# Seven-product steps from batch 5 on, one last pass for the leftover tokens of batches 4 to 7, four sums per operand, attention issued up to batch 5

## The chip, the cores and the metric

The kernel runs on one core of one Trainium2 chip. The metric is the device time of one execution in microseconds (us); lower is better. The kernel before takes 695.51 us, the median of 694.57, 695.51 and 696.79. The profile is of one further execution of 693.6 us.

## The reference

Attention over 32 memory slots, and a feed-forward layer on its output, all in fp32:

```python
a = softmax(phi, over seq)                      # 8 batches, 8 heads, 576 tokens, 32 slots
k_m, v_m = einsum('bhsm,bhsd->bhmd', a, k), einsum('bhsm,bhsd->bhmd', a, v)
p = softmax(q @ k_m.T / sqrt(64), over slots)   # 576 x 32 per head
x = (p @ v_m) laid out as 4608 tokens x 512     # 8 heads x 64
h = x @ w_in                                    # 512 -> 2048
out = gelu(h) @ w_out                           # 2048 -> 512
```

## The kernel before

A product in fp32 is made of three matmuls in the format fp32r: each operand x is split into a high part hi (a cast) and a low part lo (x - hi), and hi*hi, hi*lo and lo*hi are added up in PSUM. `copy` (line 244) makes the high parts, VectorE's subtractions the low ones. x itself is never formed: U = v_m @ w_in (`pu`, line 629, then `U` hi and lo, lines 901 and 904) is computed per batch, and the hidden layer is p @ U (`hidden`, line 945: 12 matmuls of 288 columns for 128 hidden features f of half a batch).

From batch 2 on, the work is cut into steps (batch b, half hf of its 576 tokens, pair i of the 16 blocks f). A step computes the two hidden blocks 2i and 2i+1, ScalarE applies the gelu, and one step later TensorE multiplies by the two blocks of w_out. 256 of a half's 288 tokens go through the step; the other 32 are kept in the tile `tails`. There are two kinds of product:

- A plain one (`project_half`, P): 12 matmuls of 512 columns into `acc`, fed by `gh` (the high part) and `gl` (line 977).
- A seven-product one (`seven`, S, line 1194; batches 6 and 7): Strassen's scheme on 2 x 2 blocks of 128 tokens by 256 columns. Seven products of sums of blocks, 21 matmuls of 256 columns, take the place of eight products. The sums of the gelu's blocks are made in the step on VectorE (`differences`), split by `split_hi` and `split_lo`, and `combine` adds the seven accumulators up into the output. The sums of w_out's blocks (`ws`, `wt`, `wh`, `wl`, `wz`: sum, combinations, high part, low part, store; 16 pieces spread over batches 3 to 5) are parked in DRAM, reloaded by `wi`, and `wc` swaps parts of w_out itself for its sums and back.

The leftover tokens of two batches (128 in all) go through `tg`, `tp` and `to` (split, 48 matmuls of 512 columns, output) behind batches 1, 3, 5 and 7.

The order is written out by hand. The list `START` names each piece up to batch 3 in order; behind it, `put(t, ...)` says at which half step t (32 to a batch; batch 4 is t = 128 to 159) a piece of the attention or of the weight sums is issued, `run(t)` issues what is due among the hidden blocks and gelus, and edges ("order") keep that order on each engine. A piece of step t also waits for the hidden block of half step t - 4. In names, `score` to `pl` are the attention softmax, `Up`, `Uh`, `Ul` make U, `uo` and `ui` park and reload U of batch 7, `amax` to `anorm` and `slots` prepare the memory slots of a batch. Every DMA of these stages is issued by SyncE (SP), in order.

## Time and profile before

| What | Value |
|---|---|
| median of 3 runs | 695.51 us (694.57 to 696.79) |
| profiled execution, its span | 693.6 us, 691.6 us |
| mean granted TensorE clock | 0.992 |
| TensorE busy, weight loads | 675.8 us (98%), 575.5 us (83%) |
| VectorE, ScalarE, GpSimd busy | 434.4 (63%), 375.8 (54%), 45.6 us (7%) |
| moved by DMA | 102.20 MB, mean 148 GB/s |
| chain that ended last | TensorE 88%, DMA 6%, ScalarE 2%, VectorE 2% |

Busy time says how much work an engine has; where an engine is busy all the time the others wait for it, if the chain of waits runs through it. Matmuls overlap in the pipeline, so the time of one in a group (390 ns at 512 columns) is longer than the distance between two; that distance is read from the length of a run of them in the chain, divided by their number. A granted clock of 1.00 is 2.4 GHz.

### The profile page before, as it was taken

To read this page: it belongs to the slowest core of one execution; us is meant where nothing else is said; L and a number is where in the kernel's file an instruction comes from. 1 tells how busy PE (TensorE), PEld (TensorE's weight loads), DVE (VectorE), ACT (ScalarE), POOL (GpSimd) and SP (SyncE) were. 2 spreads that over 40 slices of the span, in tenths; PEclk is the share of its full clock that TensorE was granted. 3 is DMA by queue.
4 is the path that set the end of the run, shared out by engine and by line. 5 is a ranking of instruction groups with operands and counts; after the bars stand their busy time and mean duration, and the time that the engine had idled before them with its cause. 6 is when DMAs were issued, how large, how long until landed. Compare 5 with 4: busy or idle time off the path is not lost.

```text
span 691.6 us, 13389 instructions
## 1 busy us (share of the span) xinstructions
PE 675.8 (98%) x5230; PEld 575.5 (83%) x5230; DVE 434.4 (63%) x850; ACT 375.8 (54%) x920; POOL 45.6 (7%) x38
## 2 busy tenths in 40 slices
...
GB/s 332 371 299 109 117 192 133 50 147 171 38 211 155 84 209 1 66 164 195 233 92 69 128 69 72 145 70 199 335 366 74 269 113 63 153 63 31 65 149 107
DMA packets 69378, 102.20 MB, mean 148 GB/s; under 512 B 5572, under 2 KB 43204, under 8 KB 68292
## 3 DMA queue, kind: packets, MB, share of 16 engines
...
q8 instruction: 42, 0.69, 0.4%
q14 instruction: 20, 0.16, 0.1%
...
HBM read 73.01 MB, written 28.32 MB: 147 GB/s over the span
## 4 chain that ended last, share of the span: by engine, by line
PE 88%; DMA 6%; ACT 2%; DVE 2%; issue 1%; SPq 1%; ACTq 0%; DVEq 0%
PE acc L990 35%; PE h L945 27%; PE m L1194 12%; PE tacc L990 6%; PE pu L629 4%; DMA kv<-kv 3%; PE psc L629 1%; DMA raw<-w_in 1%; DMA park<-cvr 1%; PE psc L546 1%; DMA phi<-phiT 1%; PE x L546 1%; DVE nm L436 0%; DVE gl L977 0%; DVE raw L328 0%
## 5 line engine op out<-in xcount | busy, mean ns | idle before, releaser
L945 PE MATMUL h<-p_hi,U 128*128 128x288 f32 x896 | 179.4, 299 | 0.8 <-ACT tails L964 0.5
L945 PEld LDWEIGHTS h<-p_hi,U 128*128 128x128 f32 x896 | 142.2, 188 | 21.3 <-issue 6.5
L990 PE MATMUL acc<-wo_hi,gh 128*128 128x512 f32 x384 | 150.9, 393 | 0.3 <-DVE o L244 0.2
L990 PE MATMUL acc<-wo_lo,gh 128*128 128x512 f32 x384 | 149.8, 390 | 0.0
L990 PE MATMUL acc<-wo_hi,gl 128*128 128x512 f32 x384 | 149.8, 390 | 0.0
L962 ACT ACTIVATE gf<-h 128x256 f32<-128x256 f32 x128 | 49.3, 387 | 127.5 <-PE h L945 98.7
L977 DVE TENSOR_TENSOR gl<-gf,gh 128x512 fp32r<-128x512 f32 x96 | 68.0, 710 | 58.1 <-ACT gh L244 52.4
L945 PE MATMUL h<-p_lo,U 128*128 128x288 f32 x448 | 95.4, 294 | 0.0
L990 PEld LDWEIGHTS acc<-wo_hi,gh 128*128 128x128 f32 x384 | 72.4, 188 | 17.3 <-ACT gh L244 2.5
L990 PEld LDWEIGHTS acc<-wo_hi,gl 128*128 128x128 f32 x384 | 72.1, 188 | 15.6 <-DVE gl L977 0.2
L990 PEld LDWEIGHTS acc<-wo_lo,gh 128*128 128x128 f32 x384 | 72.1, 188 | 11.9
L945 PEld LDWEIGHTS h<-p_lo,U 128*128 128x128 f32 x448 | 71.2, 188 | 0.2 <-DVE p_lo L750 0.2
L959 ACT ACTIVATE x<-h 128x256 f32<-128x256 f32 x64 | 24.6, 385 | 57.4 <-PE h L945 57.0
L904 DVE TENSOR_TENSOR U<-pu,U 128x512 fp32r<-128x512 f32 (+2 forms) x44 | 35.9, 833 | 26.6 <-ACT U L244 26.6
L1142 DVE TENSOR_TENSOR x<-x 128x256 f32<-128x256 f32 x32 | 13.6, 425 | 46.4 <-ACT x L959 46.4
L244 ACT CAST gh<-gf 128x512 fp32r<-128x512 f32 x68 | 42.4, 623 | 0.0
L1149 ACT CAST hi<-x 128x512 fp32r<-128x512 f32 x64 | 33.7, 568 | 13.5 <-DVE x L1142 13.5
L1154 DVE TENSOR_TENSOR lo<-x,hi 128x512 fp32r<-128x512 f32 x64 | 37.1, 622 | 4.8 <-ACT hi L1149 1.5
L964 ACT ACTIVATE tails<-h 128x32 f32<-128x32 f32 x192 | 37.6, 196 | 0.0
L244 ACT CAST U<-pu 128x512 fp32r<-128x512 f32 (+2 forms) x41 | 27.7, 702 | 16.0 <-PE pu L629 11.2
L1194 PE MATMUL m<-wo_lo,hi 128*128 128x256 f32 x128 | 36.1, 282 | 0.0
L1194 PE MATMUL m<-wo_hi,lo 128*128 128x256 f32 x128 | 36.1, 282 | 0.0
(159 smaller groups left out, 1086.7 us busy)
## 6 DMA issues: line engine op xcount, KB each, us to landing
...
```

What stands on the lines that cost most here:

```text
L244: return e.copy(dst, src) if e is nc.scalar else e.tensor_copy(dst, src)
L629: nc.tensor.matmul(ps[g][M * j : M * j + M], st["kT", b][rows, t, M * j : M * j + M], moving[j][rows], start=True, stop=True,)
L904: nc.vector.tensor_sub(u[:, ..., 1, :], pu, u[:, ..., 0, :].bitcast(F32))
L945: i = nc.tensor.matmul(h[:, :HS], u[g][w], x[:, g, :], start=(n == 0), stop=(n == 3 * G - 1))
L959: nc.scalar.activation(x, h[:, :n].rearrange("p (a n) -> p a n", a=2), AF.Gelu)
L962: nc.scalar.activation(gf[:, f % 2 * n : f % 2 * n + n], h[:, :n], AF.Gelu)
L964: nc.scalar.activation(t, h[:, n:HS], AF.Gelu)
L977: nc.vector.tensor_tensor(g_of("gl", *k), g_of("gf", *k), g_of("gh", *k).bitcast(F32), op=ALU.subtract)
L990: nc.tensor.matmul(acc, x, w[:, f, :], start=(first and n == 0), stop=(last and n == 2))
L1149: nc.scalar.copy(split_of("hi", b, hf, i, part), x)
L1154: nc.vector.tensor_tensor(lo, x, hi.bitcast(F32), op=ALU.subtract)
L1194: nc.tensor.matmul(acc, x, y, start=(i == 0 and k == 0 and n % 2 == 0), stop=(i == NP - 1 and k == 2), skip_group_check=True,)
```

## The change

Seven-product steps begin at batch 5, half 0 (`PS` = 10, in units of half a batch). The leftover tokens of batches 4 to 7, 256 of them, are kept (batches 6 and 7 in the tile U4) and go through a last pass of 8 seven-product steps, called batch 8: `gx` copies them into blocks on ScalarE, `combine` has six parts there and stores the quarters from two DMA queues. The scheme has four sums per operand now, not five, and fewer combinations at the end. The high and low parts of w_out share a tile `wo`, so that one of the seven products takes hi*hi and hi*lo in one matmul of 512 columns. The sums of w_out come in 8 pieces of 1024 columns, five of them written into `START` (batches 2 and 3), one each at t = 114, 140 and 147; only the right half of every second block of w_out is overwritten (`wc`, behind products of batch 4, half 1), and nothing is swapped back. The attention of all batches is issued by t = 155, U of batch 5 by t = 161: p of batches 5 to 7 and U of 6 and 7 are parked in DRAM (`po`, `uo`) and come back (`pi`, `ui`). The output copy of a plain half is on ScalarE alone from batch 3 on. The first row of the diff is one of the many rows of `START` that change.

```diff
+h.2.8.0 ws.1 wt.1 Lkv.4.1.2 Lkv.4.1.0 h.2.9.0 Lkv.4.1.4 gelu.2.8.0 Lkv.4.1.3 slotsT.3 Lkv.4.0.0
...
-    BS = 6
+    PS = 10
+    LAST_P = 4
+    LAST_U = 5
+    EARLY, OA = 8, 2
...
+            if 2 * b + hf >= PS:
                 x = blocks(b, hf, f // 2)
-                x = x[:, 2:9:6] if f % 2 else x[:, 0:2]
...
+    SUM_U = (3, "U3", "U4")
+    def w_place(i):
+        tag = SUM_U[1 + (i >= SUM_U[0])]
+        x = tile_of(
+            ("cv", tag), lambda: sb.tile([P, 2, 4, HD], F32R, tag=tag, name=f"cv_{tag}", bufs=1)
+        )
+        return x, x.bitcast(F32)
+    def w_sum(i):
+        x = w_place(i)[1]
...
+            w[:, 2 * i : 2 * i + 2].bitcast(F32).rearrange("p f n -> p (f n)")
...
+        nc.vector.tensor_tensor(x[:, 0].rearrange("p k n -> p (k n)"), hi, lo, op=ALU.add)
+    def w_sum_next(i):
+        x = w_place(i)[1]
+        w, t = x[:, 0], x[:, 1]
+        nc.vector.tensor_tensor(t[:, 0], w[:, 1], w[:, 0], op=ALU.subtract)
+        nc.vector.tensor_tensor(t[:, 2], w[:, 1], w[:, 3], op=ALU.add)
+        nc.vector.tensor_tensor(t[:, 1], w[:, 3], t[:, 0], op=ALU.add)
+        nc.vector.tensor_tensor(t[:, 3], w[:, 2], t[:, 1], op=ALU.subtract)
+    def w_sum_hi(i):
+        x, y = w_place(i)
+        nc.scalar.copy(x[:, 0], y[:, 1])
+    def w_sum_lo(i):
+        x, y = w_place(i)
+        nc.vector.tensor_tensor(x[:, 1], y[:, 1], y[:, 0], op=ALU.subtract)
+    def w_sum_out(i):
+        x = w_place(i)[1]
+        nc.sync.dma_start(park1[:, i], x[:, :, 0])
...
+            nc.sync.dma_start(park3[:, 3 * i : 3 * i + 3, w], x[:, w, 1:4])
+    def w_change(k):
+        for w, t in enumerate((wo_hi, wo_lo)):
+            t = t.bitcast(F32).rearrange("p (i x) n -> p i x n", x=2)[:, 2 * k : 2 * k + 2, 0, HD:]
+            nc.sync.dma_start(t, park1[:, 2 * k : 2 * k + 2, w])
...
+    def from_tails(i):
+        x = blocks(B, 0, i)
+        for n, t in ((0, tails(B - 1)), (1, tails(B - 3))):
+            t = t[:, 2 * i : 2 * i + 2].rearrange("p f x n -> p f (x n)")
+            if n:
+                nc.scalar.copy(x[:, 1], t[:, 0])
+                nc.scalar.copy(x[:, 0], t[:, 1])
+            else:
+                nc.scalar.copy(x[:, 2:5:2], t)
+    def differences(b, hf, i):
...
+        nc.vector.tensor_tensor(
+            x[:, 5:7], x[:, 1:2].to_broadcast([P, 2, P]), x[:, 0:3:2], op=ALU.subtract
+        )
+        nc.vector.tensor_tensor(x[:, 7], x[:, 2], x[:, 5], op=ALU.subtract)
+        nc.vector.tensor_tensor(x[:, 8], x[:, 4], x[:, 7], op=ALU.subtract)
...
         list7 = (
-            (0, 0, w(a, 1)), (0, 1, w(e, 0)), (0, 2, w(a, 0)), (0, 3, w(e, 1)),
-            (1, 0, s(1)), (1, 1, s(2)), (1, 2, s(0)),
-        )
-        m = sums_of(b, hf)
-        for n, (part, j, ws) in enumerate(list7):
-            acc = m[n // 2][:, n % 2 * HD : n % 2 * HD + HD]
+            (0, 0, s(2), m[1][:, LO]),
+            (0, 1, w(a, 0), m[2][:, LO]),
+            (0, 2, w(e, 0), m[3][:, LO]),
+            (1, 2, s(0), m[3][:, HI]),
+            (1, 1, s(1), m[0][:, LO]),
+            (1, 0, w(a, 1), m[0][:, HI]),
+            (1, 3, w(e, 1), m[1][:, HI]),
+        )
+        seen = set()
+        order = {(B, 0): (0, 4, 5, 6, 1, 2, 3), (B, NP - 1): (1, 2, 3, 4, 5, 0, 6)}
+        for n in order.get((b, i), range(7)):
+            part, j, ws, acc = list7[n]
+            bank = (1, 2, 3, 3, 0, 0, 1)[n]
             hi, lo = (split_of(v, b, hf, i, part)[:, j] for v in ("hi", "lo"))
-            for k, (x, y) in enumerate(((hi, ws[0]), (hi, ws[1]), (lo, ws[0]))):
+            three = ((acc, hi, ws[0]), (acc, hi, ws[1]), (acc, lo, ws[0]))
+            if n == 1:
+                three = ((m[2], hi, wo[:, :, a, LO]), (acc, lo, ws[0]))
+            for k, (d, x, y) in enumerate(three):
                 nc.tensor.matmul(
-                    acc, x, y,
-                    start=(i == 0 and k == 0 and n % 2 == 0),
-                    stop=(i == NP - 1 and k == 2),
+                    d, x, y,
+                    start=(i == 0 and k == 0 and bank not in seen),
+                    stop=(i == NP - 1 and k == len(three) - 1),
                     skip_group_check=True,
                 )
+            seen.add(bank)
...
+        q = o.rearrange("p a (k n) -> p (a k) n", k=2)
+        def twice(x):
+            return x.unsqueeze(1).to_broadcast([P, 2, HD])
+        def halves(x):
+            return x.rearrange("p (k n) -> p k n", k=2)
...
+            y = st["y1", b, hf] = sb.tile([P, HD], F32, tag="cols", name=f"y1_{b}_{hf}", bufs=1)
+            nc.scalar.copy(y, m[2][:, LO])
+            nc.vector.tensor_tensor(y, y, m[2][:, HI], op=ALU.add)
+        if part == 1:
+            nc.vector.tensor_tensor(q[:, 2:4], twice(st["y1", b, hf]), halves(m[3]), op=ALU.add)
+        if part == 2:
+            nc.vector.tensor_tensor(q[:, 0:4:3], twice(q[:, 3]), halves(m[0]), op=ALU.add)
+        if part == 3:
+            nc.vector.tensor_tensor(q[:, 1], q[:, 0], m[0][:, HI], op=ALU.add)
+        if b == B and part:
+            for e, k, x in ((1, 2, None), (3, 1, None), (4, 0, m[1][:, LO]), (5, 3, m[1][:, HI])):
+                if e != part:
+                    continue
+                if x is not None:
+                    nc.vector.tensor_tensor(q[:, k], q[:, k], x, op=ALU.add)
+                rows = out[(4 + k // 2 * 2) * S :][: 2 * S].rearrange("(x s) n -> x s n", s=HS)
+                rows = rows[:, 2 * P :, k % 2 * HD :][:, :, :HD]
+                by = (nc.sync, nc.scalar)[k != 2 and k != 0]
+                for y in range(2 if x is not None else 1):
+                    n = 2 if x is not None else 4
+                    by.dma_start(rows[n * y : n * y + n], q[M * n * y : M * n * (y + 1), k])
...
+        if part == 4:
+            nc.vector.tensor_tensor(q[:, 0:4:3], q[:, 0:4:3], halves(m[1]), op=ALU.add)
+            r = b * S + hf * HS
+            nc.sync.dma_start(out[r : r + 2 * P, :].rearrange("(c p) n -> p c n", p=P), o)
...
-    for b, ts in ((4, (123, 129)), (5, (150, 162)), (6, (185, 192))):
+    for b, ts in ((3, (92, 104)), (4, (119, 130)), (5, (152, 160)), (6, (138, 142)), (7, (149, 155))):
         for i, t in zip((0, 2), ts):
             put(t, f"Up.{b}.{4 * i}.4", f"Up.{b}.{4 * i + 4}.4")
             for k in range(2):
-                put(t + k, f"Uh.{b}.{4 * (i + k)}")
-                put(t + k * 1, f"Ul.{b}.{4 * (i + k)}")
-    for b, t, tq in ((4, 114, 99), (5, 142, 136), (6, 160, 152), (7, 184, 179)):
+                put(t + k, f"Uh.{b}.{4 * (i + k)}", f"Ul.{b}.{4 * (i + k)}")
...
+        (6, 133, 129, (1, 3, (0, 1, 1, 4, 4, 6, 6, 7), (1, 1, 3, 5, 6, 7, 7, 8))),
+        (7, 146, 140, (1, 3, (0, 1, 1, 3, 4, 6, 7, 7), (0, 1, 2, 3, 6, 6, 7, 8))),
...
+            if b > LAST_P:
+                put(t + lo, f"po.{b}.{hf}")
...
+            put(t + km, *heads("km", b + 2))
+    for b in range(LAST_P + 1, B):
+        for hf in range(2):
+            put(32 * b + 16 * hf - 5, f"pi.{b}.{hf}")
+    for b in range(LAST_U + 1, B):
+        for i in range(NFB):
+            put(32 * b - 16 + 4 * i + 5, f"ui.{b}.{i}")
+    put(107, "wh.4", "wl.4", "wz.4")
+    put(114, "ws.5", "wt.5")
+    put(116, "wh.5", "wl.5", "wz.5")
+    put(140, "ws.6", "wt.6")
+    put(142, "wh.6", "wl.6", "wz.6")
+    put(147, "ws.7")
+    put(148, "wt.7")
+    put(149, "wh.7", "wl.7", "wz.7")
+    put(158, *(f"wi.{k}" for k in range(IN_KV)))
+    put(159, f"wi.{IN_KV}", f"wi.{IN_KV + 1}")
+    put(162, f"wi.{IN_KV + 2}", f"wi.{IN_KV + 3}")
...
+    def ready(*k):
+        k = ".".join(map(str, k))
+        dos(f"gc.{k}.0", f"gd.{k}", f"gc.{k}.1", f"gm.{k}.0", f"gm.{k}.1")
+    def end_of(b, hf):
+        behind.append(f"C.{b}.{hf}.0")
+        behind.append(f"C.{b}.{hf}.1")
+        later.extend([[f"C.{b}.{hf}.2"], [f"C.{b}.{hf}.3"], [f"C.{b}.{hf}.4"]])
...
+        elif 2 * b + hf < PS:
             behind = [f"P.{step}"]
+            if 2 * b + hf == PS - 1 and f % 4 == 2:
+                behind += [f"wc.{f // 4}"]
             if end:
-                behind += [f"O.{b}.{hf}.{j}" for j in range(2)]
+                behind += [f"O.{b}.{hf}.{j}" + ":a" * (b > OA) for j in range(2)]
         else:
             behind = [f"S.{step}"]
-            if b == B - 1 and hf and f % 4 == 2:
-                behind += [f"wc.{f // 4}.0"]
             if end:
-                behind += [f"C.{b}.{hf}.0"]
-                later = [[f"C.{b}.{hf}.1"], [f"C.{b}.{hf}.2"], [f"C.{b}.{hf}.3", f"C.{b}.{hf}.4"]]
-        if end and b % 2 and (f == NF - 1 or b > 1 and hf):
+                end_of(b, hf)
+        if end and b in (1, 3) and (f == NF - 1 or b > 1 and hf):
             for i in range(NFB):
-                dos(f"tg.{b}.{i}")
+                dos(f"tg.{b}.{i}" + ":a" * (b > OA))
                 dos(*behind)
-                if i and later:
-                    dos(*later.pop(0))
                 behind = [f"tp.{b}.{i}"]
-                if b == BS - 1:
-                    behind += [f"wc.{i}.1"]
             behind += [f"to.{b}"]
-    dos(*behind)
+        if (b, hf, f) == (B - 1, 1, EARLY):
+            dos("gx.0")
+            ready(B, 0, 0)
+    for i in range(1, NP + 1):
+        if i < NP:
+            dos(f"gx.{i}")
+            ready(B, 0, i)
+        dos(*behind)
+        if later:
+            dos(*later.pop(0))
+        behind = [f"S.{B}.0.{i - 1}"]
+    dos(*behind, *(f"C.{B}.0.{k}" for k in range(6)))
```

Three places of the order, before and after. On TensorE, the first seven-product step of a half, of batch 6 before (`m` the accumulators; `hi`, `lo` the split sums of the gelu's blocks; `sum` the sums of w_out):

```order
L1194 MATMUL m_0_6170<-wo_hi,hi_0_0_0_6103 128x256
L1194 MATMUL m_0_6170<-wo_lo,hi_0_0_0_6103 128x256
L1194 MATMUL m_0_6170<-wo_hi,lo_0_0_0_6109 128x256
L1194 MATMUL m_0_2_6171<-sum_5677,hi_0_0_1_6107 128x256 x2
L1194 MATMUL m_0_2_6171<-sum_5677,lo_0_0_1_6111 128x256
L1194 MATMUL m_0_2_6171<-sum_5679,hi_0_0_1_6107 128x256 x2
L1194 MATMUL m_0_2_6171<-sum_5679,lo_0_0_1_6111 128x256
L1194 MATMUL m_0_3_6172<-sum_5675,hi_0_0_1_6107 128x256 x2
L1194 MATMUL m_0_3_6172<-sum_5675,lo_0_0_1_6111 128x256
```

and of batch 5 after:

```order
L1259 MATMUL m_0_5520<-sum_5370,hi_0_0_0_5453 128x256 x2
L1259 MATMUL m_0_5520<-sum_5370,lo_0_0_0_5460 128x256
L1259 MATMUL m_0_2_5521<-wo,hi_0_0_0_5453 128x512
L1259 MATMUL m_0_2_5521<-wo,lo_0_0_0_5460 128x256
L1259 MATMUL m_0_3_5522<-wo,hi_0_0_0_5453 128x256 x2
L1259 MATMUL m_0_3_5522<-wo,lo_0_0_0_5460 128x256
L1259 MATMUL m_0_3_5522<-sum_5366,hi_0_0_1_5458 128x256 x2
L1259 MATMUL m_0_3_5522<-sum_5366,lo_0_0_1_5462 128x256
L1259 MATMUL m_0_5520<-sum_5368,hi_0_0_1_5458 128x256 x2
L1259 MATMUL m_0_5520<-sum_5368,lo_0_0_1_5462 128x256
```

The products with sums come first now, and one matmul of 512 columns stands for two of 256. The accumulators are written in another order.

On VectorE, batch 4, half 0: from the low part of pair 4 (`gl_0_4`) to that of pair 6 before (in `gl_0_4` the half and the pair; `cvf` and `cvr` are the weight-sum tiles):

```order
L977 TENSOR_TENSOR gl_0_4_4486<-gf_0_4_4466,gh_0_4_4484 128x512
L1063 TENSOR_TENSOR cvr_1_4488<-cvf_1_4442,cvr_1_4488 128x5x128
L977 TENSOR_TENSOR gl_0_5_4526<-gf_0_5_4509,gh_0_5_4524 128x512
L1049 TENSOR_TENSOR cvf_0_4528<-wo_hi,wo_lo 128x512
L1053 TENSOR_TENSOR cvf_0_4528<-cvf_0_4528 128x256
L1054 TENSOR_TENSOR cvf_0_4528<-cvf_0_4528 128x256
L1055 TENSOR_TENSOR cvf_0_4528<-cvf_0_4528 128x128
L977 TENSOR_TENSOR gl_0_6_4566<-gf_0_6_4552,gh_0_6_4564 128x512
```

and after, the last twelve instructions ahead of and with the low part of pair 6 (`sT`, `smx`, `pT` belong to the softmax, `pout` is p and `Uout` U to be parked, `cv_U` the weight-sum tile; ahead of these stand, behind `gl_0_4`, two rows of each softmax sum with their two short pieces, one scaling, `gl_0_5` and two `Uout`):

```order
L928 TENSOR_TENSOR Uout_1_1_1_4697<-pu_4_1_4685,Uout_1_1_0_4696 128x512
L817 STREAM_TRANSPOSE pT_0_4727<-sT_0_4560 128x576
L811 TENSOR_TENSOR sT_1_4588<-sT_1_4588,smx_1_4702 128x576
L858 TENSOR_TENSOR pout_0_0_1_4760<-pT_0_4727,pout_0_0_0_4729 128x288
L858 TENSOR_TENSOR pout_0_1_1_4762<-pT_0_4727,pout_0_1_0_4731 128x288
L817 STREAM_TRANSPOSE pT_1_4768<-sT_1_4588 128x576
L1096 TENSOR_TENSOR cv_U_3363<-wo 128x1024
L1101 TENSOR_TENSOR cv_U_3363<-cv_U_3363 128x256
L1102 TENSOR_TENSOR cv_U_3363<-cv_U_3363 128x256
L1103 TENSOR_TENSOR cv_U_3363<-cv_U_3363 128x256
L1104 TENSOR_TENSOR cv_U_3363<-cv_U_3363 128x256
L1008 TENSOR_TENSOR gl_0_6_4796<-gf_0_6_4753,gh_0_6_4794 128x512
```

The second half of a softmax, four instructions of U, two of p and one large weight sum stand where two small pieces of a weight sum stood.

On SyncE's queue, the loads of the sums before (`parkb` keeps the parts of w_out that will be swapped):

```order
L1082 DMA parkb<-wo_hi 128x2x256 x2
L1082 DMA parkb<-wo_lo 128x2x256 x2
L1098 DMA sum_5675<-park_140 128x512
L1098 DMA sum_5677<-park_140 128x512
```

and after, the loads of p of batch 5, part of the parking of U of batch 7, a change of w_out and the first loads of sums:

```order
L840 DMA parkp_148<-pout_1_1_1_5241 128x288
L845 DMA p_hi_0_5291<-parkp_143 128x576
L845 DMA p_lo_0_5293<-parkp_143 128x576
L1145 DMA parku_142<-Uout_2_0_0_5269 128x512
...
L1145 DMA parku_142<-Uout_3_1_1_5286 128x512
L1124 DMA wo<-park_140 128x2x256 x2
L1133 DMA sum_5366<-park_139 128x512
L1133 DMA sum_5368<-park_139 128x512
```

The parking of U and p, the change of w_out and the loads of sums share one stretch of the queue; before, the changes of w_out stood behind the loads.

## Rows read from the trace of the kernel before

**Rows 1.** The page, part 1: busy time, share of the span and instructions of each engine.
```profile
PE 675.8 (98%) x5230; PEld 575.5 (83%) x5230; DVE 434.4 (63%) x850; ACT 375.8 (54%) x920; POOL 45.6 (7%) x38
```

**Rows 2.** Stretches: length, busy time per engine (instructions), granted clock, DMA share, GB/s.
```profile
340.00:420.00 80.00, 79.18 (x561) 65.68 (x560) 47.25 (x87) 39.61 (x99) 0.00 (x0) 1.00 0.30 95
460.00:480.00 20.00, 20.00 (x133) 16.39 (x132) 19.53 (x38) 15.05 (x35) 0.00 (x0) 1.00 0.44 151
480.00:500.00 20.00, 20.00 (x133) 16.43 (x132) 8.02 (x13) 9.77 (x27) 0.00 (x0) 1.00 0.94 317
500.00:520.00 20.00, 20.00 (x159) 15.84 (x158) 7.26 (x12) 7.48 (x23) 0.00 (x0) 1.00 1.04 367
560.00:660.00 100.00, 100.00 (x810) 100.00 (x808) 59.24 (x142) 52.58 (x157) 0.00 (x0) 1.00 0.20 70
```

**Rows 3.** The chain of waits in time: start us, us, engine, tile, line, instructions.
```profile
523.10 2.72 PE acc L990 x12
...
541.78 1.88 PE pu L629 x32
...
576.00 1.59 PE h L945 x12
577.60 2.49 PE m L1194 x21
...
676.56 10.92 PE tacc L990 x48
```

**Rows 4.** Timeline of the end: start us, us, engine, line, operation, output and inputs.
```profile
687.08 0.39 PE L990 MATMUL tacc<-wo_hi,gl_t 128*128 128x512 f32 x1
687.50 0.58 ACT L244 COPY to<-tacc 128x512 f32<-128x512 f32 x1 [10.40 <-PE tacc L990]
688.12 0.83 SPq L1275 DMA_DIRECT2D out<-to  x2
```

**Rows 5.** Groups on VectorE, shapes apart: count | busy us, mean ns | idle before.
```profile
L977 DVE TENSOR_TENSOR gl<-gf,gh 128x512 fp32r<-128x512 f32 x96 | 68.0, 710 | 58.1 <-ACT gh L244 52.4 <-PE pu L629 3.6
...
L1154 DVE TENSOR_TENSOR lo<-x,hi 128x512 fp32r<-128x512 f32 x32 | 22.2, 693 | 4.8 <-ACT hi L1149 1.5
L904 DVE TENSOR_TENSOR U<-pu,U 128x1024 fp32r<-128x1024 f32 x16 | 19.6, 1225 | 14.7 <-ACT U L244 14.7
L1154 DVE TENSOR_TENSOR lo<-x,hi 128x384 fp32r<-128x384 f32 x32 | 17.6, 552 | 0.0
...
L1142 DVE TENSOR_TENSOR x<-x 128x256 f32<-128x256 f32 x32 | 13.6, 425 | 46.4 <-ACT x L959 46.4
...
L807 DVE TENSOR_TENSOR sT<-sT,smx 128x576 f32<-128x576 f32 x14 | 10.6, 754 | 0.3
L795 DVE TENSOR_REDUCE smx<-sT 128x18 f32<-128x576 f32 x14 | 10.5, 749 | 3.3 <-ACT sT L791 3.2
...
L813 DVE STREAM_TRANSPOSE pT<-sT 128x576 f32<-128x576 f32 x14 | 10.3, 760 | 0.1
L1145 DVE TENSOR_TENSOR x<-x 128x128 f32<-128x128 f32 x32 | 9.1, 285 | 0.0
...
L901 DVE TENSOR_TENSOR Uout<-pu,Uout 128x512 fp32r<-128x512 f32 x8 | 5.0, 683 | 3.9 <-ACT Uout L244 3.9
```

**Rows 6.** Timeline of VectorE, batch 4: start us, us, engine, line, operation.
```profile
463.19 0.69 DVE L977 TENSOR_TENSOR gl<-gf,gh 128x512 fp32r<-128x512 f32 x1
...
473.12 0.68 DVE L977 TENSOR_TENSOR gl<-gf,gh 128x512 fp32r<-128x512 f32 x1
```

**Rows 7.** Groups on ScalarE, and one row of its timeline from 340 on.
```profile
L442 ACT ACTIVATE phi<-phi,nm 128x576 f32<-128x576 f32 x16 | 12.4, 774 | 0.7 <-DVE nm L436 0.3
...
L442 ACT ACT_TABLE_LOAD x9 | 11.5, 1283 | 0.2
...
L519 ACT ACTIVATE aT<-aT 128x1152 f32<-128x1152 f32 x6 | 6.9, 1155 | 0.0
```
```profile
345.26 0.73 ACT L1059 CAST cvr<-cvf 128x640 fp32r<-128x640 f32 x1 [4.31 <-DMA park<-cvr]
```

More of the change, by code (lines that the diff above doesn't have):

```diff
@@ L831, in p_tile, with p_part, p_out, p_in @@
         )
+    def p_part(w, b, hf, g):
+        n = 4 * hf + 2 * g + w
+        return tile_of(
+            ("pout", w, b, hf, g),
+            lambda: sb.tile([P, HS], F32R, tag=f"kv{n}", name=f"pout_{b}_{hf}_{g}_{w}", bufs=1),
+        )
+    def p_out(b, hf):
+        for g in range(G):
+            for w in range(2):
+                nc.sync.dma_start(parkp[b, hf][:, w, g], p_part(w, b, hf, g).bitcast(F32))
+    def p_in(b, hf):
+        for w in range(2):
+            t = p_tile(("p_hi", "p_lo")[w], b, hf)
+            nc.sync.dma_start(t.bitcast(F32), parkp[b, hf][:, w])
     def p_hi(b, hf, *g):
+        if b > LAST_P:
+            for x in range(G):
+                copy("a", p_part(0, b, hf, x), st["pT", b, hf][:, x])
+            return
         g = both(*g)
@@ L837, in p_lo @@
     def p_lo(b, hf, *g):
+        if b > LAST_P:
+            for x in range(G):
+                nc.vector.tensor_tensor(
+                    p_part(1, b, hf, x),
+                    st["pT", b, hf][:, x],
+                    p_part(0, b, hf, x).bitcast(F32),
+                    op=ALU.subtract,
+                )
+            return
         g = both(*g)
@@ new lines, in slot_attention_gelu_ffn @@
+    parku = [
+        dram.tile([NFB, P, G * 2 * FB], F32, tag=f"parku{b}", name=f"parku{b}", bufs=1)
+        for b in range(LAST_U + 1, B)
+    ]
+    parkp = {
+        (b, hf): dram.tile([P, 2, G, HS], F32, tag=f"parkp{b}{hf}", name=f"parkp{b}{hf}", bufs=1)
+        for b in range(LAST_P + 1, B)
+        for hf in range(2)
+    }
+    SUM_U = (3, "U3", "U4")
[5 more added lines that the diff above has]
+        return x, x.bitcast(F32)
@@ L1173, in sums_of @@
         return tile_of(("m", b, hf), make)
+    LO, HI = slice(0, HD), slice(HD, DM)
     def seven(b, hf, i):
         def w(f, half):
-            return [x[:, f, half * HD : half * HD + HD] for x in (wo_hi, wo_lo)]
+            return [x[:, f, (LO, HI)[half]] for x in (wo_hi, wo_lo)]
         def s(k):
@@ L1271, in tail_evict @@
         copy("a", o, st["tacc", b])
-        if b == B - 1:
-            for x in range(4):
-                r = (b - 1) * S + x * HS + 2 * P
-                (nc.scalar, nc.sync)[x % 2].dma_start(out[r : r + M, :], o[M * x : M * x + M])
-            return
         if b > 1:
```

374 lines of the change are left out of this document (139 added, 235 removed), and 2 rows, old and new, of the table t.

## Prediction

> **What bounds the kernel now.** I read the busy shares first: TensorE is busy 675.8 us of the span of 691.6, VectorE 434.4, ScalarE 375.8 [rows 1]. So time can come out only where TensorE's own work shrinks, and it can go in only where TensorE is made to wait. Then the stretches [rows 2]: in 340 to 420 TensorE lacks 0.82 us of 80; from 460 to 520 it lacks nothing, though VectorE is 19.53 of 20 busy in the first 20 us and the DMA engines are at 317 and 367 GB/s in the other 40; from 560 to 660 it lacks nothing, with the granted clock at 1.00 (of 2.4 GHz). Third, the chain of waits [rows 3]: it runs through TensorE alone there, one step's 12 hidden matmuls (1.59) and one step's product in turn. A plain product is 12 matmuls in 2.72 us, 0.2267 each at 512 columns; a seven-product step is 21 in 2.49, 0.1186 each at 256 columns. Last the end [rows 4]: from the end of the last matmul (687.47) there is one copy of 0.58 on ScalarE, then the issue of the last store at 688.12; the span ends 3.5 us behind that.
>
> **The change, part by part.** All sums are against the profiled execution (693.6 us, span 691.6) and are then set off from the median, 695.51.
>
> Products. The new seven-product step is 19 matmuls of 256 columns and one of 512: 19 x 0.1186 + 0.2267 = 2.48 us. Batch 5 has 16 steps that go from 2.72 to 2.48: -3.84. Batches 6 and 7 have 32 steps from 2.49 to 2.48: -0.3. The leftover tokens of batches 4 to 7 cost two passes of 48 matmuls now: 10.92 each (the second of them stands in the chain [rows 3]); in their place stand 8 steps of 2.48 = 19.84: -2.0. Together **-6.2 us**, all of it on the path. The number of attention and hidden matmuls is the same, and only their place changes.
>
> The Trainium skill has a rule against these spacings: "TensorE: Matmul & The Clock Gate", section "Back-to-back issue gap", gives N/2.4 + 2.5 ns for an isolated gap, thus 109 ns at 256 columns and 216 ns at 512, where the rows show 119 and 227. By the rule the step is 19 x 0.109 + 0.216 = 2.29, a plain step 2.59, a leftover pass 20.7 for both batch pairs, and the gain 4.8 + 2.4 = 7.2 (estimates from that page); the rows decide, and my sum stays with 6.2.
>
> End. The last matmuls no longer feed one copy. Behind them come one ScalarE copy and a row of additions on VectorE, of 256 and of 512 columns: y, then two of 512, three of 256, most of them one after the other on the same tile. The last pass orders its products so that the accumulators of the first additions close early; I count the last product's addition, and what of the earlier chain is not done by then, as four pieces of 256 columns at 0.425 [rows 5]: 1.7, against the 0.58 now. Term **+1.1** (-0.2 if only one addition is late, +2.5 if all of the chain is); the stores then take their 3.5 us as before.
>
> Batch 4, first half. Attention of batch 6 and a weight sum now stand in VectorE's queue ahead of the low part of pair 6 (gl, line 1008), for which the product waits. Between the low parts of pairs 4 and 6 stand, by rows 5: two softmax sums (2 x 0.75) with two short pieces each (4 x 0.285 at most), two scalings (2 x 0.754), two transposes (2 x 0.76), four low parts of U (4 x 0.683), two of p (2 x 0.43), gl of pair 5 (0.71), the weight sum of 1024 columns (1.225), four of its combinations at 256 columns (4 x 0.425), and gl of pair 6 itself (0.71): 13.6 us. TensorE has in that time two plain products, two sets of hidden matmuls and one U product: 2 x 2.72 + 2 x 1.59 + 1.88 = 10.5 [rows 3], and about 0.9 of lead. So gl comes 2.2 us late by lengths laid end to end. But they overlap a little: a like run of 17 instructions, from one gl to the next but one, took 9.93 us (463.19 to 473.12 [rows 6]), where the mean lengths of its groups add up to some 11.0, nine tenths. Nine tenths of 13.6 are 12.3, 0.9 more than TensorE's cover: **+0.9**, bounds 0 (row 460 to 480, where a full VectorE stopped nothing) and 2.2.
>
> Batch 3. The exponential block of ScalarE (table 1.283, two of 0.774, 1.155, table 1.283 [rows 7]) gets one more cast of 1024 columns, which I price as the 1152-column exponential, 1.155: 6.4 in all, ahead of the gelu of pair 6; a second such block follows in the second half. TensorE's cover is a plain step of 4.31 [rows 3] and the slot products, which I put at about one (a fraction of the U product's 1.88): some 5.5. **+1.0** for the two (0.3 to 1.5). In exchange the 0.82 that TensorE lacks in 340 to 420 goes: in that stretch a weight-sum cast waits 4.31 us for its parking DMA with gelus queued behind it [rows 7], and the old pieces of those sums are gone from there: **-0.8** (0 to -0.8).
>
> Batch 2. Weight sums 0 to 2 are now pinned into its steps; no wait of TensorE is seen near, and a piece of 1024 columns can hold a low part up by its own length. **+0.2**, bounds 0 and 1.2.
>
> Last pass. Its steps last 2.48 us, not 4.08, since there are no hidden matmuls left. VectorE's part of a step is 0.425 + 2 x 0.285 + 0.693 + 0.552 = 2.24 [rows 5]; ScalarE's, at the 52.58 us that 100 us of such steps (24.5) cost it now, 2.15 [rows 2]. Both fit, but they wait for each other within a step, so the loop may be as long as 2.7. One step is prepared early. **+0.3** (0 to 1.8).
>
> Nothing is put down for the change of halves, where the outputs are read out of PSUM in fewer pieces than now beside the next half's hidden matmuls, nor for the eviction on ScalarE, which is busy 54% of the span [rows 1].
>
> DMA. U of batches 6 and 7 and p of batches 5 to 7 are parked and come back. From the second half of batch 4 to batch 5's third seven-product step I count 4.2 MB of U out, 1.2 of p out, 0.6 of p in, 2.1 into the weights, 6.3 of sums in, 0.5 of output: 14.9 MB. TensorE has six plain steps, two U products and two seven-product steps in that time, 6 x 4.31 + 2 x 1.88 + 2 x 4.07 = 37.8 us, so 394 GB/s are asked for. Rows 2 show 317 and 367 for a pair of such stretches with TensorE never idle. The first eight sums are asked for two plain steps before their use and need about half of that, so I take **0**; if the whole queue were the limit at the mean 342 GB/s, 14.9 MB last 43.6: +5.8.
>
> On this the Trainium skill speaks against the change: "DMA: Bandwidth & Descriptors", section "Specifications", puts the HBM limit of one core at about 358 GB/s, below what is asked for. Row 500 to 520 shows 367 for reads and writes together, so the ceiling is about there; by the page's figure the same bytes take 41.6 us, 3.8 more than TensorE's work; if nothing could be late without harm, rival C below would give 695.8 by it.
>
> Sum: -6.2 + 1.1 + 0.9 + 1.0 - 0.8 + 0.2 + 0.3 = -3.5 us; from the median 695.5 that is **692.0 us** (690.1 against the profiled 693.6, which lies 1.9 below the median; the difference is carried over, not the level).
>
> **The rivals.** *A, all of it hidden.* VectorE's queue has slack that I don't see, as in 460 to 480, and only the end is paid: -6.2 - 0.8 + 1.1 = -5.9, 689.6 us. Against it: gl of pair 6 is queued behind more VectorE work than there is TensorE work beside it.
> *B, no change: the attention that moves into fewer batches is paid for in waits.* Batch 4, batch 3, batch 2 and the last pass at the upper part of their bounds, 2.2 + 1.5 + 0.4 + 1.0, with the end: -5.9 + 5.1 = -0.8, 694.7. For it: attention and sums of the last three batches now have to be done two batches earlier, on engines that were already full once (19.53 of 20).
> *C, slower: the DMA queue is the bound before batch 5.* One queue carries the parked U, the parked p, the changed weights and the sums in order, and the changed weights wait for the products that still read them. If the first sums arrive more than about 4 us later than I count (the lead at two plain steps, less the transfer), the first seven-product step stands still, and the delay reaches the whole difference, 5.8. Then -3.5 + 5.8 = +2.3, 697.8. For it: 394 asked for against 367 at most; against it: later loads in the queue may be late for free.
> That the seven-product steps do not pay at all is excluded by the two rows of 2.72 and 2.49.
>
> **How the numbers follow.** Forecast 0.45, A 0.16, B 0.22, C 0.17. A difference of over 0.3%, 2.1 us, can be told from no change, so faster is below 693.4. The forecast's own range, 690.6 to 693.6, lies mostly there: 0.39 faster, 0.06 same. With A, faster is 0.55. B is 0.20 same and 0.02 slower, C 0.15 slower and 0.02 same: same 0.28, slower 0.17. The range that holds 8 in 10 goes from a little under A, 689.3, to a little over C, 698.2.
>
> **What would show it.** Right: steps of line 1259 at 2.48 us and eight of them in a row at the end, in batch 5 a step of 4.07; TensorE's idle time of about 1 us each in batch 3 and in the first half of batch 4, ahead of the product of pair 6, released by gl; the last store issued some 1.8 us behind the last matmul. Wrong: a wait of a line 1259 matmul for a sum's DMA at the start of batch 5 (C); waits of several microseconds at many places of batches 2 to 4 (B); none but at the end (A); a product of 512 columns into two accumulator halves that is longer than 0.227.

## The result, and the profile after

The changed kernel takes 703.39 us, the median of four runs (702.36 to 703.85), against 695.83 for the kernel before (four runs): a ratio of 1.0108 with a 95% interval of 1.0088 to 1.0128, so 7.6 us slower. The forecast was 692.0, 3.5 us faster. The profiled execution has a span of 700.4 us.

The busy shares of the changed kernel, the page's first part, which answer to [rows 1]:

```profile
PE 675.3 (96%) x5390; PEld 581.2 (83%) x5390; DVE 461.8 (66%) x909; ACT 397.4 (57%) x978; POOL 45.6 (7%) x38
```

TensorE's busy time is all but the same, 675.3 us against 675.8, though it has fewer columns to multiply. So it was slower somewhere, and the span grew by 8.8 us beside it. The stretches (length, busy time of PE, PEld, DVE, ACT and POOL, granted clock, DMA share, GB/s), which answer to [rows 2]:

```profile
300.00:320.00 20.00, 17.86 (x162) 14.08 (x165) 9.95 (x18) 9.31 (x22) 0.00 (x0) 0.91 0.89 295
400.00:420.00 20.00, 20.00 (x153) 14.83 (x152) 12.86 (x24) 12.33 (x31) 0.00 (x0) 1.00 0.41 140
460.00:480.00 20.00, 19.32 (x141) 16.05 (x141) 10.45 (x20) 11.15 (x31) 0.00 (x0) 1.00 1.00 367
680.00:700.40 20.40, 7.66 (x62) 7.31 (x60) 7.96 (x17) 3.99 (x11) 0.00 (x0) 0.79 0.09 27
```

Two of these rows are not full. In 300 to 320 TensorE lacks 2.14 us and the clock is granted at 0.91; in the last 20.4 us it works for 7.66 only. From 400 to 420, where pair 6 of batch 4's first half lies, it lacks nothing, though the forecast had put 0.9 us there. From 460 to 480 it lacks 0.68.

The chain of waits of the changed kernel (start us, us, engine, tile, line, instructions), which answers to [rows 3]:

```profile
558.97 1.59 PE h L976 x12
560.56 2.50 PE m L1259 x20
...
572.84 2.45 PE m L1259 x20
...
662.59 25.08 PE m L1259 x200
```

A seven-product step of 20 matmuls takes 2.45 to 2.50 us, on the mean as long as one of 21 did, and with its hidden matmuls (1.59; six for each of its two blocks, twelve in all) it is 4.08 as before. The last ten steps stand together in 25.08, so the last pass of eight is 20.06 us.

The end of the changed kernel, a timeline (start us, us, engine, line, operation) that answers to [rows 4]:

```profile
687.18 3.25 SPq L1301 DMA_DIRECT2D out<-o  x3
...
687.38 0.28 PE L1259 MATMUL m<-wo,lo 128*128 128x256 f32 x1
687.70 0.69 DVE L1287 TENSOR_TENSOR o<-o,m 128x512 f32<-128x512 f32 x1 [0.54 <-PE m L1259]
...
688.87 2.46 ACTq L1301 DMA_DIRECT2D out<-o  x3
688.87 0.75 DVE L1295 TENSOR_TENSOR o<-o,m 128x256 f32<-128x256 f32 x2
```

The last matmul starts at 687.38 and ends at 687.66, 0.2 us later than the last one before. VectorE's additions end at 689.62, the last store is issued at 691.33, and the span ends at 700.4. So the tail behind the last matmul is 12.7 us where it was 4.1: 1.35 us more until the last sum is there (1.96, not 0.61), and 7.3 us more from there to the end (10.8, not 3.5). Two questions follow: why are the stores so slow, and where did TensorE's own gain go?

For the stores, the DMA view of the last stretch, of the changed kernel and then of the kernel before (40 equal slices of the stretch, with the busy share of the 16 DMA engines in tenths and the rate, then the issues with their size and, for some, the time to landing; ScalarE's queue has as many in the changed kernel as SyncE's, of the same sizes):

```profile
DMA  0000000000022221222111111111111111110000
GB/s 0 0 0 0 0 0 0 0 0 0 10 30 80 100 95 40 67 87 85 25 7 27 35 20 35 35 40 50 50 45 50 47 47 50 47 47 25 0 0 0
...
out<-o SPq DMA_DIRECT2D x1, 128.0 KB
...
out<-o SPq DMA_DIRECT2D x2, 64.0 KB
...
```

```profile
DMA  0000000299999950000000000069979700000000
GB/s 0 0 0 0 0 0 0 108 431 388 399 453 366 431 184 0 0 0 0 0 0 0 0 0 0 0 172 216 248 248 302 183 11 0 0 0 0 0 0 0
...
out<-o SPq DMA_DIRECT2D x1, 512.0 KB
out<-to SPq DMA_DIRECT2D x2, 64.0 KB, 1.7
out<-to ACTq DMA_DIRECT2D x2, 64.0 KB, 2.0
```

Half a megabyte goes out at up to 100 GB/s first and at 20 to 50 for most of the time in the changed kernel; a quarter goes out at 170 to 300 in the kernel before (its second burst; the first is the store of a half). The share goes with the rate: 2 tenths of the 16 DMA engines are at work after while the two stores of four groups go out, 1 tenth for the stores of two groups, 6 to 9 before. The stores differ in shape: one group of 32 rows per store before, two or four groups of 32 half rows after. That a single large store can be fast shows in the first burst before: the half's 512 KB are one store, whose slowest dimension is the 128 partitions, and it runs at up to 453 GB/s.

For TensorE, the waits of the changed kernel (us in total, times, longest) and the rows on both sides of the longest, SyncE's queue and TensorE:

```profile
PE psc L630 <- DMA q<-qT: 2.3, 2, 2.1
...
PE h L976 <- ACT tails L995: 0.7, 1, 0.7
...
PE acc L1021 <- DVE gl L1008: 0.2, 1, 0.2
```

```profile
303.84 3.17 SPq L393 DMA_DIRECT2D kv<-kv  x4
...
308.28 0.34 SPq L424 DMA_DIRECT2D q<-qT  x1
```

```profile
314.75 2.52 PE L630 MATMUL psc<-q,kT 64*32 64x288 f32 x32 [2.12 <-DMA q<-qT]
317.20 3.17 PE L547 MATMUL psc<-kv,aT 128*32 128x128 f32 x64
```

The loads of q of batch 4 are issued at 308.28, behind eight loads of keys and values of 256 KB (four of them are shown), and the scores wait for them until 314.75. What follows is slow: 32 score matmuls take 2.52 us and 64 of the slots 3.17. The same in the kernel before:

```profile
309.68 0.33 SPq L423 DMA_DIRECT2D q<-qT  x1
```

```profile
325.64 1.20 PE L629 MATMUL psc<-q,kT 64*32 64x288 f32 x32
326.77 1.96 PE L546 MATMUL psc<-kv,aT 128*32 128x128 f32 x64
```

There q is issued at 309.68, no earlier, but the scores begin at 325.64, 16 us later, and take 1.20 and 1.96. The change moved the scores six half steps forward (t = 108, not 114) and asked for q earlier in the table too (t = 94, not 99); but the hand-written list reaches further than that time, so the loads came first behind its last entry, batch 6's values, as they had before.

### The profile page after: what moved, and what is told of

Read it like the earlier page. It is cut to its first block, busy times and chain, and to the rows that moved or that the text cites. A ratio compares the mean times of both kernels' runs of the same rounds, so it can differ in the third digit from the quotient of the medians.

```text
span 700.4 us, 13888 instructions
## 1 busy us (share of the span) xinstructions
PE 675.3 (96%) x5390; PEld 581.2 (83%) x5390; DVE 461.8 (66%) x909; ACT 397.4 (57%) x978; POOL 45.6 (7%) x38
## 4 chain that ended last, share of the span: by engine, by line
PE 87%; DMA 5%; DVE 3%; ACT 2%; issue 1%; SPq 0%; DVEq 0%; ACTq 0%
PE acc L1021 28%; PE h L976 27%; PE m L1259 20%; PE pu L630 4%; PE tacc L1021 3%; DMA q<-qT 2%; DMA parkp<-pout 1%; PE psc L630 1%; PE psc L547 1%; DMA kv<-kv 1%; PE pk L572 1%; DMA parku<-Uout 1%; PE pt L468 1%; DMA phi<-phiT 1%; PE x L547 1%
## 5 line engine op out<-in xcount | busy, mean ns | idle before, releaser
L1021 PE MATMUL acc<-wo,gh 128*128 128x512 f32 x640 | 198.9, 392 | 0.0
L1021 PEld LDWEIGHTS acc<-wo,gh 128*128 128x128 f32 x640 | 116.0, 188 | 24.8 <-issue 1.4
L1021 PE MATMUL acc<-wo,gl 128*128 128x512 f32 x320 | 125.1, 391 | 0.2 <-DVE gl L1008 0.2
L1202 ACT CAST hi<-x 128x384 fp32r<-128x384 f32 x112 | 63.6, 567 | 37.3 <-DVE x L1195 36.1
L1259 PE MATMUL m<-wo,hi 128*128 128x512 f32 (+1 forms) x392 | 84.6, 298 | 0.0
L1206 DVE TENSOR_TENSOR lo<-x,hi 128x384 fp32r<-128x384 f32 x112 | 69.6, 621 | 12.6 <-ACT hi L1202 12.4
L1021 PEld LDWEIGHTS acc<-wo,gl 128*128 128x128 f32 x320 | 60.1, 188 | 14.1 <-DVE gl L1008 1.3
L1259 PE MATMUL m<-sum,hi 128*128 128x256 f32 x336 | 64.8, 282 | 0.0
L1259 PEld LDWEIGHTS m<-wo,hi 128*128 128x128 f32 x392 | 62.5, 190 | 2.4 <-DVE o L1285 0.2
L1259 PE MATMUL m<-wo,lo 128*128 128x256 f32 x224 | 63.2, 282 | 0.0
```

The source lines that it names most:

```text
L1021: nc.tensor.matmul(acc, x, w[:, f, :], start=(first and n == 0), stop=(last and n == 2))
L1202: nc.scalar.copy(split_of("hi", b, hf, i, part), source(b, hf, i, part))
L1206: nc.vector.tensor_tensor(lo, source(b, hf, i, part), hi.bitcast(F32), op=ALU.subtract)
L1259: nc.tensor.matmul(d, x, y, start=(i == 0 and k == 0 and bank not in seen), stop=(i == NP - 1 and k == len(three) - 1), skip_group_check=True,
```

## The experiments

The theory: two losses, each of its own. The last stores are slow because several groups of 32 rows are in one store (some 7 us), and q comes late, with a lower clock behind the wait (some 5 us). The rivals: the additions or the number of stores make the tail; the loads are late by the bandwidth, whatever their order; the lower clock has another reason; the attention in fewer batches costs more waits, hidden now (rival B of the prediction).

**e1, the stores by 32 rows.**

```diff
-                for y in range(2 if x is not None else 1):
-                    n = 2 if x is not None else 4
-                    by.dma_start(rows[n * y : n * y + n], q[M * n * y : M * n * (y + 1), k])
+                for y in range(4):
+                    by.dma_start(rows[y], q[M * y : M * y + M, k])
```

> The changed kernel, whose last stores of the leftover tokens are cut into 16 pieces of 32 rows x 256 columns (one group of 32 tokens each) in place of six pieces of 4 or 2 groups. Theory (the rows of one store with an outer dimension of 2 or 4 go out one after the other, 46 ns each): the tail from the last matmul to the end falls from 12.8 to about 5.5 us, the time by 6 to 8, to 696. Rival 1 (the additions on VectorE and the number of stores make the tail): no gain, or slower by some 2 us, since there are ten more issues. Rival 2 (the queue for q and its clock make all of it): within 1 us of 703.4.

696.13 us. Since each group of kernels ran beside its own runs of the kernel before (694.3 us here, 695.8 with the changed kernel), they are compared by their ratios to it: 1.0019 (1.0005 to 1.0034), 0.9% or 6.2 us under the changed kernel's 1.0108, with ten stores more. The end of this kernel's timeline, and its DMA view:

```profile
689.13 3.69 ACTq L1300 DMA_DIRECT2D out<-o  x8
689.13 0.75 DVE L1295 TENSOR_TENSOR o<-o,m 128x256 f32<-128x256 f32 x2
```

```profile
GB/s 0 0 0 0 0 0 0 0 0 0 0 0 0 0 0 34 87 90 30 117 26 98 120 90 151 177 79 196 83 188 38 83 90 30 117 4 0 0 0 0
...
out<-o SPq DMA_DIRECT2D x8, 32.0 KB, 1.6
```

The additions are where they were, the stores land in 1.6 us, and the tail is 7.0 us, 5.8 less. The rivals of additions and of issues fall. So does the theory's own way to the slow stores: rows of 1 KB one after the other, 46 ns each, would be 22 GB/s, and the stores of four groups had run at up to 100.

**e4 and e8, the store's shape on the kernel before.** e4 makes its last four stores one store of four groups; e8 leaves them as four, but puts all on SyncE's queue.

```diff
-            for x in range(4):
-                r = (b - 1) * S + x * HS + 2 * P
-                (nc.scalar, nc.sync)[x % 2].dma_start(out[r : r + M, :], o[M * x : M * x + M])
-            return
+            rows = out[(b - 1) * S : (b + 1) * S].rearrange("(x s) n -> x s n", s=HS)
+            nc.sync.dma_start(rows[:, 2 * P :], o)
+            return
...
-                (nc.scalar, nc.sync)[x % 2].dma_start(out[r : r + M, :], o[M * x : M * x + M])
+                nc.sync.dma_start(out[r : r + M, :], o[M * x : M * x + M])
```

> The kernel before, whose last store (four pieces of 32 rows x 512 columns on two queues) is one store of 4 groups of 32 rows on one queue. Theory (such a store is slow by its shape): 4 to 6 us slower, 700, at the same last matmul. Rival 1 (the shape is of no account): the same time, or 0.4 us faster for the fewer issues.

> The kernel before, with its last four stores of 32 rows all on one queue (two on each before). Theory (the number of token groups within one store makes it slow, not the queue): within 1 us of the kernel before. Rival (what cost 4 us in e4 was that one queue carried all): 3 to 4 us slower, as e4.

e4: 698.33 us, ratio 1.0056 (1.0033 to 1.0078), 3.9 us slower. e8: 695.89, ratio 1.0022 (1.0006 to 1.0039), 1.5 us slower, half a microsecond over what was expected. By the two traces e4's tail is 3.1 us longer than before and e8's only 0.7; the rest of e8's loss lies elsewhere, in its profile in a wait of TensorE of 2.25 us at 350 (0.52 before). So it is the groups in one store, and of the queue at most the 0.7. The DMA view of e4's end:

```profile
DMA  0000001999950000000004132012222222200000
GB/s 0 0 0 0 0 0 74 435 391 421 384 185 0 0 0 0 0 0 0 0 22 52 7 15 15 7 52 59 81 103 103 103 103 103 89 30 0 0 0 0
...
out<-to SPq DMA_DIRECT2D x1, 256.0 KB
```

The store runs at some 100 GB/s, and at less than half of that at first; four of a group each had run at 170 to 300. At 103 GB/s two tenths of the DMA engines are busy (a quarter would read 2), where the four stores had 6 to 9. The kernel before had shown this in its own middle, where it cost nothing: the store of the leftover tokens of batches 2 and 3 has this shape. Its DMA view of 381 to 387:

```profile
GB/s 0 0 0 0 0 14 68 41 27 0 14 14 14 14 14 0 55 177 55 55 96 82 109 109 109 96 96 109 109 82 109 96 82 14 0 0 0 14 263 352
...
out<-to SPq DMA_DIRECT2D x1, 256.0 KB
```

256 KB, alone on the queue until 385.8, go out slowly at first and then at about 100 GB/s, as in e4. That was there to be read for the forecast.

**e2, q early.** The loads of q of batch 4 stand in the list ahead of weight sum 3, at the start of batch 3.

```diff
-O.2.1.0 h.3.2.0 ws.3 wt.3 O.2.1.1 h.3.3.0
+O.2.1.0 Lq.4.0 Lq.4.1 h.3.2.0 ws.3 wt.3 O.2.1.1 h.3.3.0
```

> The changed kernel with the loads of q of batch 4 issued at the start of batch 3, ahead of a weight sum's parking and of batch 6's keys and values. Theory (q is late because it stands behind 2.6 MB of loads, and the wait costs 2.1 us and the slow clock behind it about 3 more): 5 us faster, 698.3, no stretch at the lower clock in batch 3. Rival 1 (the transfers are late because the DMA engines are full there, so the next load is late in its place): within 1.5 us. Rival 2 (the lower clock has nothing to do with the wait): 2 us faster, and the clock still falls.

698.41 us, ratio 1.0059 (1.004 to 1.0078): 0.5% or 3.4 us under the changed kernel, between the theory's 5 and rival 2's 2. TensorE at the scores and the slots, and the stretch around it:

```profile
313.22 1.20 PE L630 MATMUL psc<-q,kT 64*32 64x288 f32 x32
314.37 1.96 PE L547 MATMUL psc<-kv,aT 128*32 128x128 f32 x64
```

```profile
300.00:320.00 20.00, 20.00 (x219) 16.85 (x204) 12.53 (x25) 10.54 (x26) 0.00 (x0) 1.00 0.74 232
```

The scores begin 1.5 us sooner and take 1.20, the slots 1.96, as in the kernel before, and the granted clock is 1.00 all through. So 2.12 us of waiting, 1.32 of the scores and 1.21 of the slots are saved there, 4.65 together: the 0.91 of the changed kernel (some 3.6 us of the 20 at the lower level, 1.2 GHz) belongs to the wait, and rival 2 falls. About one of the 4.65 is given back at the end of batch 4, where TensorE waits longer than the 0.68 us of the changed kernel:

```profile
460.10 0.53 PE L976 MATMUL h<-p_hi,U 128*128 128x288 f32 x2 [1.63 <-ACT tails L995]
```

Why it is longer there was not tested; e6 to e9 are about that place.

**e10, the early scores on the kernel before.** Only t of the attention of batch 4.

```diff
-    for b, t, tq in ((4, 114, 99), (5, 142, 136), (6, 160, 152), (7, 184, 179)):
+    for b, t, tq in ((4, 108, 99), (5, 142, 136), (6, 160, 152), (7, 184, 179)):
```

> The kernel before, with the attention of batch 4 six half steps earlier (t = 108, not 114), as the changed kernel has it, and nothing else. Theory (the loads of q stand where they stood, so the scores wait for them and the clock falls): TensorE waits 1.5 to 2.5 us for q in batch 3, a stretch at the lower clock follows, 3.5 to 5.5 us slower than the kernel before. Rival (it is the changed kernel's larger parking of weight sums that makes q late): no wait for q, within 1 us of the kernel before.

> Once more the kernel before with the attention of batch 4 six half steps earlier, since the profile taken of it (1697 us, TensorE slow from the first to the last stage) can't be read. Theory: TensorE waits 1.5 to 2.5 us for q in batch 3, a stretch at the lower clock follows, 3.5 to 5.5 us slower than the kernel before. Rival: no wait for q; where the time is over 10 us longer, the waits lie at other places, since attention of batch 4 meets a weight sum or U there.

The two are one kernel: ratios 1.0185 (1.0166 to 1.0204) and 1.0183 (1.0153 to 1.0212), some 13 us slower, far more than the theory asked for. The shift also changes values behind the scores, so the total isn't used, and only the stretch up to them is read, in the second profile. SyncE's issue of q, TensorE, and the stretch around it:

```profile
309.81 0.33 SPq L423 DMA_DIRECT2D q<-qT  x1
```

```profile
315.93 1.88 PE L629 MATMUL psc<-q,kT 64*32 64x288 f32 x24 [3.24 <-DMA q<-qT]
318.09 1.18 PE L629 MATMUL psc<-q,kT 64*32 64x288 f32 x8 [0.28 <-DMA q<-qT]
```

```profile
300.00:320.00 20.00, 16.48 (x123) 12.39 (x125) 7.26 (x15) 3.91 (x14) 0.00 (x0) 0.91 0.79 247
```

q is issued when it was issued before, the scores wait 3.5 us for it, 24 of them take 1.88, and the granted clock is 0.91. So the early scores alone make this wait, without the larger weight sums. Behind it stand two more waits of this kernel, 4.4 and 1.0 us for an output copy and a low part, which the changed kernel does not have.

**e3, both edits.** e1 and e2 together.

> Both edits, the stores by 32 rows and the early q. Theory (the two losses are all that went wrong, and are independent): 703.4 - 7 - 5 = 691 us, faster than the kernel before by 4 to 5. Rival (the attention in fewer batches costs waits that come up once these are gone): 694 to 697.

694.00 us, ratio 0.9982 (0.9967 to 0.9997). By the ratios the two gains, 0.9% and 0.5%, should give 0.997, and it is 0.998, so they add up within the intervals. The 691 us that were expected asked for 7 and 5 us; e1 brought 6.2 and e2 3.4. By the ratio the kernel is faster than the one before by 0.2%, 1.2 us (the two medians lie 0.3 apart), which is less than the 0.3% that the forecast counts as a change. The rival (694 to 697) named the number better; a wait of 1.25 us at 459 fits its mechanism.

**e5, whole rows.** On top of e3, the last outputs go out as 8 stores of 32 whole rows, two on each queue per half of the groups, once both column halves are there.

```diff
+                if x is None:
+                    continue
...
-                rows = rows[:, 2 * P :, k % 2 * HD :][:, :, :HD]
-                by = (nc.sync, nc.scalar)[k != 2 and k != 0]
...
+                for y in range(4):
+                    (nc.sync, nc.scalar)[y % 2].dma_start(
+                        rows[y, 2 * P :], o[M * y : M * y + M, k // 2]
+                    )
```

> e3_both, with the last outputs stored as 8 pieces of 32 whole rows (512 columns) in place of 16 half rows, four per token group half, two on each queue. Theory (after the shape is mended, the rest of the tail of 7.1 us is the issue of 8 stores on one queue, 3.7 us behind the additions): the tail falls to some 5.3 us, the time by 1.5 to 2 against e3, 0.6% faster than the kernel before. Rival (the landing of the stores ends the tail, whatever their number): within 0.5 us of e3.

692.54 us, ratio 0.9973 (0.9959 to 0.9986): 0.6 us under e3 by the ratios, with intervals that overlap, so no more than the rival allowed. The tail is 6.3 us, down from 7.1 (5.3 was expected): 2.0 of it are the additions.

**e6, e7 and e9, where U and p of batch 7 are parked.** TensorE's last wait in the changed kernel, at the end of batch 4, has its reason in ScalarE's queue, where copies of U wait for a buffer that p's parking still reads. Its timeline in the changed kernel:

```profile
460.01 0.59 ACT L245 CAST Uout<-pu 128x512 fp32r<-128x512 f32 x1 [1.45 <-DMA parkp<-pout]
462.01 0.59 ACT L245 CAST Uout<-pu 128x512 fp32r<-128x512 f32 x1 [1.42 <-DMA parkp<-pout]
```

All three stand on e5. e6 moves the second half of U of batch 7 half a step back, e7 a whole step, with the loads of the sums behind it; e9 also splits p later.

```diff
-    for b, ts in (..., (7, (149, 155))):
+    for b, ts in (..., (7, (149, 156))):                # e6
+    for b, ts in (..., (7, (149, 157))):                # e7, e9; the first loads of sums at t = 160
...
-        (7, 146, 140, (1, 3, (0, 1, 1, 3, 4, 6, 7, 7), (0, 1, 2, 3, 6, 6, 7, 8))),
+        (7, 146, 140, (1, 3, (0, 1, 1, 3, 4, 6, 8, 8), (0, 1, 2, 3, 6, 6, 8, 9))),   # e9
```

> e5 with the second half of U of batch 7 half a step later (t = 156, not 155). Theory (its copy on ScalarE waits 3.1 us for the buffer that p's parking still reads, with a gelu queued behind it, and TensorE loses 1.25): the wait shortens by about 2 us and TensorE loses nothing there, 1.0 to 1.3 us less than e5. Rival (the parking DMA is late by the load of the whole queue, so the sums of w_out come late instead): same time as e5 or slower, with a wait at the first seven-product step.

> As e6, a whole step later (t = 157), and the first ten sum loads at t = 160. Theory of the buffer: the wait of TensorE for ScalarE is gone, as in e6. Rival (the DMA queue binds): the first seven-product step waits for its sums, 1 to 4 us slower than e6.

> e7 with the splitting of p of batch 7 a half step later (t + 8, not t + 7), behind a gelu. Theory (ScalarE's copies of p wait about a microsecond each for the parking of U, with gelus queued behind them, and TensorE loses 1.1 us for it): that wait is 0 to 0.5, the time 0.6 to 1.1 us under e7, 0.4% under the kernel before. Rival (the parking falls behind whatever is asked of it, and the next copy waits instead): the same time as e7, with the wait at the next copies.

692.22 (0.9969, 0.9958 to 0.9981), 692.78 (0.9976, 0.9961 to 0.9992) and 692.89 us (0.9972, 0.9957 to 0.9987): none differs from e5. The first of ScalarE's copies of p in e6 and TensorE behind it, the stretch around them, and then the same place in e5, which lacks e6's edit alone:

```profile
448.00 0.43 ACT L245 CAST pout<-pT 128x288 fp32r<-128x288 f32 x1 [1.37 <-DMA parku<-Uout]
...
452.82 0.53 PE L976 MATMUL h<-p_hi,U 128*128 128x288 f32 x2 [1.19 <-ACT tails L995]
...
453.81 1.95 PE L630 MATMUL pu<-w_in,kT 64*32 64x512 f32 x32
```

```profile
440.00:460.00 20.00, 18.81 (x147) 13.71 (x146) 13.06 (x21) 11.27 (x30) 0.00 (x0) 1.00 0.97 326
```

```profile
448.77 0.43 ACT L245 CAST pout<-pT 128x288 fp32r<-128x288 f32 x1 [1.39 <-DMA parku<-Uout]
449.60 1.95 PE L630 MATMUL pu<-w_in,kT 64*32 64x512 f32 x32
```

The copies of U wait no longer in e6, but TensorE loses 1.19 us at the four copies of p (1.09 in e7, 1.00 in e9). These copies are not slower than they were: they wait 0.85 to 1.37 us each for the parking of U in e6, 0.88 to 1.39 in e5, and 0.75 to 1.28 in the changed kernel. In e5 a U product stands at that place (449.60) and gives TensorE 1.9 us of work while ScalarE waits; e6 moves this product behind the wait (453.81). So the edit took one wait away, and with it the cover of another. In e9 the copies of p wait 0.6 to 0.7 us for the parking of U, over the 0 to 0.5 of its theory, and one waits 1.43 for VectorE. The first seven-product step waits for no sum in any of them, against the rivals of e6 and e7, though e6's time lies where its rival had it. With the DMA engines at 0.97 busy from 440 to 460 the parking itself has little room. e6 is the fastest kernel of the study, 0.3% under the kernel before; e5, e7 and e9 can't be told from it.

## Why the prediction was wrong

*The mechanism of the gain held, at nine tenths.* Batch 5's steps went from 4.31 to 4.08 (-3.6; -3.8 was said), the leftover passes from 21.84 to 20.06 (-1.8; -2.0), and batches 6 and 7 gave nothing (-0.3): a step of 20 matmuls takes 2.49 on the mean, as one of 21 did, and not the 2.48 of the sum. In the last pass a step takes 2.51. -5.4 in place of -6.2.

*The end is the step that failed most*: "the stores then take their 3.5 us as before". The additions were sized well (1.35 us more, +1.1 said). From the last sum to the end it took 10.8, and e1 takes 5.8 us of that away with the shape of the stores alone. The bounds of the forecast's term, -0.2 to +2.5, were bounds of the additions; for the stores no row was read, though the kernel before had one of that shape (the 100 GB/s in batch 3, which e4 shows at the end). The last store was issued 3.7 us behind the last matmul, not 1.8. The Trainium skill has the rule, and it was missed: by "DMA: Bandwidth & Descriptors", section "Why a DMA increments its semaphore by 16 and not by 1", a transfer runs on as many of the 16 engines, k, as the largest number up to 16 that divides the slowest dimension of both its sides. That makes k 4 for four groups, 2 for two and 16 for 32 rows; the busy shares of 2, of 1 and of 6 to 9 tenths agree.

*The second is a wait that the sum does not have.* The forecast asked of each moved step what stands ahead of it on VectorE and ScalarE, and of SyncE's queue only before batch 5. That the scores moved 13 us forward and the loads of q did not stood in the order of SyncE and in the trace (issue at 309.68, use at 325.64). e2 prices it at 4.65 us in place, of which 2.1 are the wait and the rest the lower clock behind it, and 3.4 in the end.

*The waits that were forecast* did not come. Batch 4's first half lost nothing (+0.9 said): gl of pair 6 was done at 421.12, just ahead of its first matmul:

```profile
420.43 0.69 DVE L1008 TENSOR_TENSOR gl<-gf,gh 128x512 fp32r<-128x512 f32 x1
...
421.20 0.46 PE L1021 MATMUL acc<-wo,gl 128*128 128x512 f32 x1
```

From the end of gl of pair 4 VectorE took 12.1 us for that (12.3 said); TensorE had 12.2 of work and lead (11.4 said). So VectorE's queue was read rightly, and a margin of 0.1 us kept the wait away. Neither did batch 3's exponential block (+1.0) stop TensorE; batch 2's 0.2 came (0.21), and TensorE has no wait in the last pass (+0.3). The 0.82 us that TensorE lacked from 340 to 420 went but for 0.16, as said.

*Rival C*, the DMA queue, was right on the sign and not on the place. 460 to 480 shows 367 GB/s with the DMA engines busy all through, as 500 to 520 had before, and e7 384 in the same stretch. By the Trainium skill, "DMA: Bandwidth & Descriptors", section "Specifications", the HBM limit of a core is about 358; the two traces lie 2.5% and 7% over it. The section "Bandwidth" of that page of the skill has 425 for a load of 16 MB on a core that runs alone, as this one does, and both lie under it. But the sums were there for the first seven-product step. What came late was the release of the parking buffers, for 0.68 us (1.0 to 1.7 in e2 to e9).

Together: -5.4 + 8.6 for the end + 4.65 for q and the clock + 0.7 at the end of batch 4 - 0.4 (0.37 of small waits in place of 0.74) = +8.2 us, against 8.8 between the two spans; the other 0.6 is not placed.

What stays open: which transfer holds up the parking at the end of batch 4 (three places for the copies were tried, and a wait of 1.0 to 1.2 us stayed), and 0.8 us of the tail that e5 has over the kernel before, beside the additions' 1.35.
